# Token and channel weights as float32 in DRAM, VectorE's normalization of the last batch, and a later w_out product

## The chip, the cores and the metric

The kernel runs on one core of one Trainium2 chip. The metric is the device time in microseconds (us) of one execution; each time given for a kernel is the median of several runs. A profile of one further execution gives the trace. In it PE is TensorE, DVE is VectorE, ACT is ScalarE, POOL is GpSimd and SP is SyncE, whose queue issues every DMA of this kernel.

## The reference

Four batches (B = 4) of 576 tokens (S), 8 heads of 64, pass through attention, then through two feed-forward blocks. The weights of the blocks come in float64.

```
scores = q @ k.T / 8; bias = -(cum_i - cum_j)            # cum = cumsum(max(s, 0))
attn = softmax(where(causal, -1e9, scores + min(bias, 0)))
x = attn @ v                                             # (B, 576, 512)
h = gelu_tanh(x @ w_in); u, v = split(h)                 # first block
v_n = (v - mean(v)) / sqrt(var(v) + 1e-6) * g_ln
x = x + (u * (w_sg @ v_n + b_sg)) @ w_out
theta = x @ w_theta                                      # second block
y = w_tok_r @ (x * cos(theta)) + w_tok_i @ (x * sin(theta))
u = x + y
out = u + max(u @ w_ch, 0)
```

## The kernel before

Every product with weights is made of three float32r matmuls, high by high, high by low and low by high, so each weight tensor is kept as a high and a low part in SBUF. A float64 weight is first turned into float32: `to32` takes one ScalarE multiplication and three VectorE operations on its bits (lines 711, 717, 718 and 720). Then `rnd` on ScalarE makes the high part (line 98), and `sub` on VectorE or GpSimd the low part (line 106).

The work has two stretches. In `attention`, pairs of heads `p` = 5 to 16 go by in stages of some 20 us: scores (`sc`), a maximum on VectorE that frees the scores' PSUM (`L417`), the exponential on ScalarE (`L428`), transposes (`T`), and the product with v (`Y`, `Z`). The first block of the batch before (`ffn_in` and `ffn_gate`) is a generator from which `pace` takes matmuls to fill TensorE between them. `PLAN` says in which stage, and at which of four places of it, a piece of a weight is loaded or converted: `R` loads and `W` converts a piece of w_out (first eight) or w_theta, and `W` stores it as float32 to the DRAM tensor `wd`. Their rooms are tiles that the filler does not need yet: `vT` in stages 8 and 12, `vl` and `vh` in stages 9 and 13.

After attention, `ffn_in(3)` and `ffn_gate(3)` of the last batch run alone, the products with w_out (`wout`, matmuls `wo`) of batches 0 and 1 fill in, that of batch 2 follows, and that of batch 3 runs with `theta(0)` (`tp`, `th`). Then `mix` runs (`yo`, `co`). `wout` loads the gated values (`gr`), splits them (`gh`, `gl`; two `gr` and six of each of the others), adds x (`xr`) and stores to `x2d`, from which `theta` loads `x2T`. Meanwhile the generator `second_weights` prepares the second block's weights, one step for every eighth step of `ffn_in(3)` and for every step of `wout`: 8 loads from `wd`, 18 pieces of the token weights (`wk`) and 8 of the channel weights (`wch`) straight from the float64 inputs through `weights64`, which converts each with `to32`. All go through three `wraw` buffers. For the last batch (`alone` in `ffn_in`), `moments` and `norm` follow each of the five row tiles of v; `norm`'s first operation is on GpSimd (line 886).

The order on an engine is set by the program's order and a scheduler that moves instructions between priorities before the kernel is built; on the chip each engine, and SP's queue, runs strictly in that order.

Of the kernel before, what the change touches and what calls it, by code (L numbers as in the profile page):

```python
# [22 lines left out]
P = 128  # L23
# [32 lines left out]
class Kernel:  # L56
# [12 lines left out]

    PLAN = {5: ("C5 L7", "C6", "G0", "C7 G1 B"), 6: ("H0 G2", "H1 G3", "H2 G4", "H3 G5"),  # L70
# [684 lines left out]
    def ffn_weights(self):  # L755
        p = self.f1
        self.wih = self.f3.tile([P, 4, DFF], F32R, name="wih")
        self.wil = self.f3.tile([P, 4, DFF], F32R, name="wil")
        self.wsh = p.tile([P, 4, S], F32R, name="wsh")
        self.wsl = p.tile([P, 4, S], F32R, name="wsl")  # L760
        self.wsrh = p.tile([P, S], F32R, name="wsrh")
        self.wsrl = p.tile([P, S], F32R, name="wsrl")
        self.bsg = p.tile([P, S], F32, name="bsg")
        self.wraw = p.tile([P, 2, FH, 2], U32, name="wraw", tag="vl")
        self.wtab = p.tile([P, 4, FH], F32, name="wtab", tag="vh")
        self.wgt = {}
# [27 lines left out]

    def convert_piece(self, kind, k):
# [6 lines left out]
        elif kind in "RW":  # L802
# [12 lines left out]
            else:  # L815
                raw, ta = self.room[k % 4]
                self.to32(raw.bitcast(U32).rearrange("p (n t) -> p n t", t=2), ta)
                nc.sync.dma_start(self.wd[k // 2, :, h * 256:h * 256 + 256], ta)
        elif kind in "GH":
# [35 lines left out]
    def ffn_in(self, b):  # L855
# [4 lines left out]
        uT = self.f1.tile([P, 4, S], F32, name="uT", tag="uT")  # L860
# [23 lines left out]
        def norm(t):  # L884
            r = TT[t][1]
            nc.gpsimd.tensor_scalar(vT[0:r, t], vT[0:r, t], rs[0:r, t:t + 1], nm[0:r, t:t + 1],  # L886
                                    op0=ALU.mult, op1=ALU.add)
            self.rnd("act", vh[0:r, t], vT[0:r, t])
            if t < 4:
                self.sub("dve", vl[:, t], vT[:, t], vh[:, t])  # L890
            else:
                self.sub("dve", vh[64:128, 4], vT[0:64, 4], vh[0:64, 4])


        for t, (a, r) in enumerate(TT):
# [21 lines left out]
            if t == 4:  # L917

                nc.scalar.copy(uT[0:64, 3, 0:512], o[64:128])
                nc.vector.tensor_tensor(vT[0:64, 4], o[0:64], uT[0:64, 3, 0:512], op=ALU.add)  # L920
# [69 lines left out]
    def wout(self, b, pool):  # L990
        nc = self.nc
        gs = []
        for ft in range(4):
# [6 lines left out]
            gs.append((gh, gl))  # L1000
        for dt in range(4):
# [130 lines left out]
    def run(self):  # L1132
        nc = self.nc
        with ExitStack() as root, ExitStack() as right2, ExitStack() as left2:
# [5 lines left out]
            self.wd = dr.tile([8, P, DM], F32, name="wd")  # L1140
            self.rd = dr.tile([B * H // 2, 2, 5 * P], F32, name="rd")
# [69 lines left out]
    def weights64(self, src, his, los, n):  # L1211

        c = n // 2
        pool = self.stg
        for i in (0, 1):
            raw = pool.tile([P, c, 2], U32, name="wraw", tag="wraw", bufs=3)
            ta = pool.tile([P, c], F32, name="wta", tag="wta", bufs=3)
            for r, w in src:
                self.nc.sync.dma_start(raw[r:r + w.shape[0]].rearrange("p n t -> p (n t)"),
                                       w[:, 2 * i * c:2 * (i + 1) * c])  # L1220
            self.split64(raw, ta, his[:, i * c:(i + 1) * c], los[:, i * c:(i + 1) * c], "pool")
            yield

    def second_weights(self):
# [6 lines left out]
        for k in range(8):  # L1231
            h, l = ((self.woh, self.wol), (self.wth, self.wtl))[k // 4]
            raw = self.stg.tile([P, DM // 2, 2], U32, name="wraw", tag="wraw", bufs=3)
            w = raw.rearrange("p n t -> p (n t)").bitcast(F32)
            self.nc.sync.dma_start(w, self.wd[k])
            self.rnd("act", h[:, k % 4], w)
            self.sub("pool", l[:, k % 4], w, h[:, k % 4])
            yield
        for i in range(9):
            if i < 8:  # L1240
                src = [(0, (self.w_tr, self.w_ti)[i % 2][i // 2 * P:(i // 2 + 1) * P])]
            else:

                src = [(0, self.w_tr[512:576]), (64, self.w_ti[512:576])]
            yield from self.weights64(src, self.wkh[:, i], self.wkl[:, i], S)
        while self.wc is None:
            yield
        self.wch = self.wc.tile([P, 4, DM], F32R, name="wch")
        self.wcl = self.wc.tile([P, 4, DM], F32R, name="wcl")
        for t in range(4):  # L1250
            yield from self.weights64([(0, self.w_ch[t * P:(t + 1) * P])], self.wch[:, t], self.wcl[:, t], DM)
# [46 lines left out]
```

## Time and profile before

| | |
|---|---|
| median of 3 runs | 654.76 us (651.64 to 655.22) |
| the profiled execution | 654.41 us, of which the span of the trace is 652.7 us |
| busy in the span | PE 623.4 us, DVE 423.0 us, ACT 354.5 us, POOL 184.4 us |
| granted TensorE clock | 0.994 of full speed |
| DMA | 83.57 MB |

A share of busy time is an average over stretches with different limits. The rows further down cut the span into stretches; a stretch in which PE is busy for less than its length has a wait in it that something else ended. Matmuls are pipelined, so a matmul's own duration is longer than the distance to the next one.

### The profile page before, as it was taken

The numbers are of one execution on the slowest core, as the hardware profiler recorded it, in microseconds if no ns is written. First come the engines' busy times: TensorE is split into PE (matmuls) and PEld (weight loads), VectorE is DVE, ScalarE is ACT, GpSimd is POOL, SyncE is SP. The second block draws the span as 40 slices with busy tenths as digits, with TensorE's granted clock in tenths as the row PEclk, the third lists the DMA queues.
The fourth block names the chain that finished last, engine by engine and source line by source line (L and its number), as shares of the span: only waits on it lengthen the run. The fifth ranks groups of instructions, "written<-read, shape, count | busy, mean of one in ns | idle before, by whom it ended". The sixth has DMA issues, their size and how long they took to land.

```text
span 652.7 us, 12650 instructions
## 1 busy us (share of the span) xinstructions
PE 623.4 (96%) x4703; PEld 545.9 (84%) x4703; DVE 423.0 (65%) x1048; ACT 354.5 (54%) x829; POOL 184.4 (28%) x213
## 2 busy tenths in 40 slices
PE   9898999899989999999997798999999999999997
PEld 6675777787778878778797797999999899989997
DVE  7896678555674575652299977887663676477422
ACT  5885788656677655771374345655440562256000
POOL 6464424343043440333596534020000100100000
PEclk9999999999999999999998899999999999999999
DMA  6777753565335552112448788621004001300101
GB/s 187 232 246 218 220 162 93 184 224 183 105 107 160 194 176 85 55 38 92 150 126 266 232 302 306 198 95 38 1 1 146 1 1 42 105 1 2 73 1 73
DMA packets 49805, 83.57 MB, mean 128 GB/s; under 512 B 7920, under 2 KB 19792, under 8 KB 49744
## 3 DMA queue, kind: packets, MB, share of 16 engines
q1 hardware_dynamic: 49744, 82.76, 39.4%
q8 instruction: 37, 0.61, 0.4%
q14 instruction: 24, 0.20, 0.1%
HBM read 61.61 MB, written 21.13 MB: 127 GB/s over the span
## 4 chain that ended last, share of the span: by engine, by line
PE 66%; DMA 9%; ACT 7%; DVE 6%; POOL 4%; issue 2%; SPq 0%; DVEq 0%; ACTq 0%; POOLq 0%
PE yo L109 17%; PE fo L109 15%; PE th L109 8%; PE co L109 8%; PE wo L109 5%; PE T L458 4%; PE Y L109 4%; PE sc L109 3%; ACT E L428 2%; POOL vT L886 2%; DMA rd<-rT 2%; DMA xT<-rd 1%; DMA x2T<-x2d 1%; PE tp L1035 1%; DMA x2d<-xr 1%
## 5 line engine op out<-in xcount | busy, mean ns | idle before, releaser
L428 ACT ACTIVATE E<-E,negm 128x192 f32<-128x192 f32 (+4 forms) x160 | 88.4, 555 | 2.7 <-DVE negm L417 2.6
L109 PE MATMUL yo<-wkh,zh 128*128 128x288 f32 x288 | 85.2, 296 | 0.2 <-DVE x2T L1108 0.2
L109 PE MATMUL yo<-wkl,zh 128*128 128x288 f32 x288 | 85.2, 296 | 0.0
L109 PE MATMUL yo<-wkh,zl 128*128 128x288 f32 x288 | 85.2, 296 | 0.0
L417 DVE CUSTOM_DVE_ANT_0 E<-sc,C 128x192 f32<-128x192 f32 (+4 forms) x160 | 68.7, 484 | 2.4 <-PE sc L109 1.6
L458 PE MATMUL T<-ident,E 128*128 128x128 f32 x400 | 55.9, 275 | 7.4 <-DVE xT L525 4.0
L109 PE MATMUL fo<-x,wih 128*128 128x288 f32 x256 | 56.6, 305 | 1.1 <-ACT uT L954 1.1
L458 PEld LDWEIGHTS T<-ident,E 128*128 128x128 f32 x400 | 45.5, 140 | 11.5 <-DVE xT L525 4.4
L102 POOL TENSOR_SCALAR xt<-x2s 128x128 fp32r<-128x128 f32 x16 | 10.8, 690 | 156.5 <-DVE x2s L106 156.5
L109 PEld LDWEIGHTS yo<-wkh,zh 128*128 128x128 f32 x288 | 54.1, 188 | 0.7 <-DVE x2T L1108 0.4
L109 PEld LDWEIGHTS yo<-wkl,zh 128*128 128x128 f32 x288 | 54.1, 188 | 0.3
L109 PEld LDWEIGHTS yo<-wkh,zl 128*128 128x128 f32 x288 | 54.0, 188 | 0.1
L109 PE MATMUL co<-u,wch 128*128 128x288 f32 x256 | 53.0, 295 | 0.0
L109 PE MATMUL wo<-gh,woh 128*128 128x288 f32 x128 | 39.2, 309 | 7.8 <-ACT gh L98 4.1
L109 PEld LDWEIGHTS fo<-x,wih 128*128 128x128 f32 x256 | 41.7, 188 | 3.6 <-ACT uT L954 1.8
L98 ACT CAST u<-x2T 128x576 fp32r<-128x576 f32 x16 | 10.7, 671 | 59.3 <-DVE x2T L1108 59.3
L109 PE MATMUL th<-wth,x2s 128*128 128x512 f32 x128 | 42.9, 400 | 0.0
L468 DVE COPY Ef<-T 128x512 f32<-128x512 f32 x32 | 22.0, 686 | 32.3 <-PE T L458 32.0
L109 PE MATMUL fo<-wih,x 128*128 128x512 f32 x128 | 42.4, 403 | 0.0
L109 PEld LDWEIGHTS co<-u,wch 128*128 128x128 f32 x256 | 41.6, 188 | 0.0
L109 PE MATMUL fo<-wsh,vh 128*128 128x288 f32 x128 | 38.8, 307 | 1.9 <-ACT wsh L98 1.9
L109 PE MATMUL sc<-kh,qh 64*128 64x288 f32 (+1 forms) x192 | 38.9, 365 | 1.3 <-DVE negm L417 1.2
(214 smaller groups left out, 1758.5 us busy)
## 6 DMA issues: line engine op xcount, KB each, us to landing
C<-cd SPq DMA_DIRECT2D x15, 576.0 KB, 4.9
xT<-rd SPq DMA_DIRECT2D x32, 144.0 KB, 3.2
xd<-xT SPq DMA_DIRECT2D x16, 288.0 KB, 4.9
gd<-uT SPq DMA_DIRECT2D x16, 288.0 KB, 2.1
gr<-gd SPq DMA_DIRECT2D x16, 288.0 KB, 4.3
xr<-xd SPq DMA_DIRECT2D x16, 288.0 KB, 3.7
x2d<-xr SPq DMA_DIRECT2D x16, 288.0 KB, 2.5
x2T<-x2d SPq DMA_DIRECT2D x4, 1152.0 KB
```

The lines of the kernel that those rows point to most:

```text
L98: nc.scalar.copy(out, src)
L102: nc.gpsimd.tensor_scalar(out, src, 1.0, 1.0, op0=ALU.mult, op1=ALU.mult)
L109: return self.nc.tensor.matmul(out, lhsT, rhs, start=start, stop=stop)
L417: self.nc.vector.tensor_tensor_reduce(at if j else at[:, ::-1], self.sc[t, j].rearrange("p (b k) -> p b k", k=64), C[:, j, 0:n].rearrange( ...
L428: self.nc.scalar.activation(at, at, AF.Exp, bias=self.negm[pr % 2][:, j, c:c + 1], scale=-1.0, accum_out=sm[:, j * 5 + c:j * 5 + c + 1])
L458: nc.tensor.transpose(T[:, col:col + P], E[:, c:c + P], self.ident)
L468: nc.vector.tensor_copy(Ef[:, 512:1024], T)
L886: nc.gpsimd.tensor_scalar(vT[0:r, t], vT[0:r, t], rs[0:r, t:t + 1], nm[0:r, t:t + 1], op0=ALU.mult, op1=ALU.add)
L1035: nc.tensor.transpose(tp[0:r, dt * P:(dt + 1) * P], x2T[:, dt, a:a + r], self.ident)
```

## The change

- `PLAN` gets pieces `M` (load) and `N` (convert, store) for the 18 pieces of the token weights: three at stage 9, three at 13, four at 15 and eight at 16. The float32 result goes to a new DRAM tensor `wkd`. The first six use the tile `uT` as room; the others use operand, score and raw-load buffers of attention.
- In `ffn_in`, the tile `uT` is therefore taken only ahead of the second half of the matmuls, and the short fifth row tile uses `vT` in place of `uT`.
- `second_weights` begins with converting the 8 channel pieces and storing them to `wcd`; then it loads 8 pieces from `wd`, 9 from `wkd` (576 wide, where there were two of 288) and 4 from `wcd`, and splits each. Its steps are taken at every sixteenth step of `ffn_in(3)` from the 64th on.
- The first operation of `norm` is on VectorE for the last batch.
- `wout` of batch 0 yields a cost of 6000 between its loads and its matmuls.

```
     PLAN = {5: ("C5 L7", "C6", "G0", "C7 G1 B"), 6: ("H0 G2", "H1 G3", "H2 G4", "H3 G5"),
             7: ("H4 G6", "H5 G7", "H6 G8", "H7 G9 H8 H9"),
-            8: ("R0 R1", "R2 R3", "W0 W1", "W2 W3"), 9: ("R4 R5", "R6 R7", "W4 W5", "W6 W7"),
-            12: ("R8 R9", "R10 R11", "W8 W9", "W10 W11"), 13: ("R12 R13", "R14 R15", "W12 W13", "W14 W15")}
+            8: ("R0 R1", "R2 R3", "W0 W1", "W2 W3"), 9: ("R4 R5 M0", "R6 R7 M1 M2", "W4 W5 N0", "W6 W7 N1 N2"),
+            12: ("R8 R9", "R10 R11", "W8 W9", "W10 W11"),
+            13: ("R12 R13 M3", "R14 R15 M4 M5", "W12 W13 N3", "W14 W15 N4 N5"),
+            15: ("M6 M7", "M8 M9", "N6 N7", "N8 N9"),
+            16: ("M10 M11 M12 M13", "N10 N11 M14 M15", "N12 N13 M16 M17", "N14 N15 N16 N17")}
...
+        elif kind == "M":
+            i, h = divmod(k, 2)
+            if k < 6:
+                if k % 3 == 0:
+                    room = self.f1.tile([P, 4 * S], F32, name="wroom", tag="uT")
...
+            for r, w in self.token_rows(i):
+                nc.sync.dma_start(raw[r:r + w.shape[0]], w[:, h * S:h * S + S])
+        elif kind == "N":
+            raw, ta = self.token.pop(k)
+            self.to32(raw.bitcast(U32).rearrange("p (n t) -> p n t", t=2), ta)
+            nc.sync.dma_start(self.wkd[k // 2, :, k % 2 * 288:k % 2 * 288 + 288], ta)
...
-        uT = self.f1.tile([P, 4, S], F32, name="uT", tag="uT")
...
-            nc.gpsimd.tensor_scalar(vT[0:r, t], vT[0:r, t], rs[0:r, t:t + 1], nm[0:r, t:t + 1],
-                                    op0=ALU.mult, op1=ALU.add)
+            (nc.vector if alone else nc.gpsimd).tensor_scalar(
+                vT[0:r, t], vT[0:r, t], rs[0:r, t:t + 1], nm[0:r, t:t + 1], op0=ALU.mult, op1=ALU.add)
...
+        uT = self.f1.tile([P, 4, S], F32, name="uT", tag="uT")
...
+        if b == 0:
+
+            yield 6000.0
...
-                    if n % 8 == 0:
+                    if n % (8 if n < 64 else 16) == 0:
                         self.later(prep)
...
+        for k in range(8):
+            t, h = divmod(k, 2)
+            raw = self.stg.tile([P, S], F32, name="wraw", tag="wraw", bufs=3)[:, 0:DM]
+            ta = self.stg.tile([P, 256], F32, name="wta", tag="wta", bufs=3)
+            nc.sync.dma_start(raw.bitcast(U32), self.w_ch[t * P:(t + 1) * P, h * DM:(h + 1) * DM])
+            self.to32(raw.bitcast(U32).rearrange("p (n t) -> p n t", t=2), ta)
+            nc.sync.dma_start(self.wcd[t, :, h * 256:h * 256 + 256], ta)
             yield
...
+        for k in range(21):
...
+            raw = self.stg.tile([P, S], F32, name="wraw", tag="wraw", bufs=3)[:, 0:n]
+            nc.sync.dma_start(raw, w)
+            self.rnd("act", h, raw)
+            self.sub("pool", l, raw, h)
             yield
```

How the scheduler places this shows in each engine's order. The first place is SP's queue around the start of `ffn_gate(3)`, where `wraw` are weight loads, `gr` and `xr` the loads of `wout`, and `gd` the stores of the gate. Before:

```order
L1219 DMA wraw<-in_moe2_w_tok_r 128x576 x2
L1219 DMA wraw<-in_moe2_w_tok_i 128x576 x2
L1219 DMA wraw<-in_moe2_w_tok_r 128x576
L995 DMA gr<-gd 128x576 x2
L1219 DMA wraw<-in_moe2_w_tok_r 128x576
L1004 DMA xr<-xd 128x576 x3
L1219 DMA wraw<-in_moe2_w_tok_i 128x576
L995 DMA gr<-gd 128x576
```

And with the change:

```order
L1284 DMA wraw<-wd 128x512 x3
L1030 DMA gr<-gd 128x576 x2
L1284 DMA wraw<-wd 128x512
L1042 DMA xr<-xd 128x576 x2
L1284 DMA wraw<-wd 128x512
L1042 DMA xr<-xd 128x576
L1284 DMA wraw<-wkd 128x576
L1030 DMA gr<-gd 128x576 x2
L1022 DMA gd<-uT 128x576
L1284 DMA wraw<-wkd 128x576 x2
```

The loads of `gr` still stand behind weight loads in the queue, but behind loads of float32 pieces, whose buffer is given back by a cast and a subtraction, where it was given back by a whole conversion.

The second place is VectorE at the end of stage 9, where `wtabs` and `wroom` are conversions, `ISA E` the maxima over the scores, and `vT<-fo` the fifth row tile of the filler. Before:

```order
L718 SCALAR_TENSOR_TENSOR wtabs<-wroom,wtabs 128x256 x2
L720 SCALAR_TENSOR_TENSOR wtabs<-wroom,wtabs 128x256
L472 COPY E_72<-T 128x512
L417 ISA E,negm_77<-sc,C 128x9x64
...
L720 SCALAR_TENSOR_TENSOR wtabs<-wroom,wtabs 128x256
L417 ISA E,negm_77<-sc,C 128x576
...
L920 TENSOR_TENSOR vT<-fo,uT 64x512
L468 COPY Ef<-T 128x512
L417 ISA E,negm_77<-sc,C 128x7x64
```

And with the change:

```order
L721 TENSOR_SCALAR wroom<-wroom 128x288
L476 COPY E_74<-T 128x512
L421 ISA E,negm_79<-sc,C 128x9x64
...
L722 SCALAR_TENSOR_TENSOR wtabs<-wroom,wtabs 128x256
L421 ISA E,negm_79<-sc,C 128x192
...
L954 TENSOR_TENSOR vT<-fo,vT 64x512
L722 SCALAR_TENSOR_TENSOR wroom<-wroom 128x288
L472 COPY Ef<-T 128x512
L721 TENSOR_SCALAR wroom<-wroom 128x288
```

Conversions (`wroom`, a token piece, and `wtabs`, a piece of w_out) now stand between the maxima of one group of scores and those of the next.

The third place is TensorE just after the first scores of stage 10, where `fo<-x` are the filler's matmuls of the second half of `ffn_in`. Before:

```order
L109 MATMUL fo<-x,wih 128x288
L109 MATMUL fo<-x,wil 128x288
L458 MATMUL T<-ident,E 128x128 x8
L109 MATMUL fo<-x,wih 128x288 x3
L109 MATMUL fo<-x,wil 128x288 x2
L109 MATMUL fo<-x,wih 128x288 x4
```

And with the change:

```order
L113 MATMUL sc<-mpick,mlow 128x64
L462 MATMUL T<-ident,E 128x128 x19
L113 MATMUL fo<-x,wih 128x288
L113 MATMUL fo<-x,wil 128x288
```

Nineteen transposes stand in a row, without the filler's matmuls that stood between them. Further on, in the last batch, the first matmul of `wout` stands behind 71 of the 112 matmuls of `ffn_gate(3)`, where it stood behind 48.

## Rows read from the trace of the kernel before

**Rows 1.** Stretches of the span: busy us of each engine (instructions), clock, DMA, GB/s.

```profile
core 0: us, PE busy (x) PEld busy (x) DVE busy (x) ACT busy (x) POOL busy (x), PEclk, DMA share, GB/s
128.00:314.70 186.70, 183.43 (x1475) 148.94 (x1473) 107.24 (x332) 113.15 (x293) 60.08 (x68) 1.00 0.38 126
314.70:340.30 25.60, 25.60 (x157) 23.11 (x153) 16.05 (x38) 15.82 (x32) 22.80 (x22) 1.00 0.51 152
340.30:369.20 28.90, 20.79 (x139) 19.63 (x137) 27.75 (x46) 13.46 (x31) 17.93 (x19) 0.94 0.74 236
369.20:400.00 30.80, 28.22 (x195) 27.05 (x195) 23.71 (x53) 13.73 (x30) 11.44 (x15) 0.95 0.92 316
400.00:450.60 50.60, 50.60 (x308) 45.46 (x309) 40.56 (x81) 30.64 (x54) 7.26 (x9) 1.00 0.46 143
```

**Rows 2.** What PE waited for from 340.3 to 400.1: us, times, longest.

```profile
PE wo L109 <- ACT gh L98: 4.1, 2, 3.3
PE wo L109 <- DVE xr L1012: 3.7, 2, 3.3
PE tp L1035 <- ACT x L1038: 1.3, 1, 1.3
PE fo L109 <- DVE vh L106: 0.9, 1, 0.9
```

**Rows 3.** A window of 5 us at the end of that stretch, columns as in rows 1.

```profile
390.00:395.00 5.00, 4.58 (x34) 4.33 (x33) 3.49 (x9) 0.89 (x3) 1.94 (x3) 1.00 1.01 380
```

**Rows 4.** The chain that ended last: start us, length, what.

```profile
387.46 9.26 DMA x2T<-x2d
...
407.48 3.18 PE wo L109 x24
```

**Rows 5.** Conversions (tile `wta`) in the stretch: busy us of DVE, ACT, POOL, then as rows 1.

```profile
340.30:369.20 28.90, 19.78 (x30) 8.59 (x21) 11.04 (x11) 0.94 0.74 236
369.20:400.00 30.80, 12.28 (x28) 7.89 (x19) 8.64 (x10) 0.95 0.92 316
```

**Rows 6.** GpSimd's normalizations (its five on `vT`): ns min/median/max, first and last start.

```profile
L886 POOL TENSOR_SCALAR vT<-vT,rs,nm x5: 782/1044/1774, 329.7 to 339.1; 128x512 f32<-128x512 f32 x4, 64x512 f32<-64x512 f32 x1
```

**Rows 7.** A group of VectorE's operations from 300 to 450: busy us, mean ns, idle before.

```profile
L1064 DVE TENSOR_SCALAR kk<-kk 128x512 f32<-128x512 f32 x7 | 3.1, 441 | 2.2 <-ACT kk L1063 2.2
```

**Rows 8.** A GpSimd and a VectorE instruction side by side: start us, length.

```profile
330.49 1.41 POOL L106 TENSOR_TENSOR wtl<-wraw,wth 128x512 fp32r<-128x512 f32 x1
...
330.77 1.44 DVE L718 SCALAR_TENSOR_TENSOR wta<-wraw,wta 128x288 uint32<-128x288 uint32 x1
```

**Rows 9.** SP's queue at the first `gr` loads: start us, length.

```profile
345.81 0.90 SPq L995 DMA_DIRECT2D gr<-gd  x2
```

**Rows 10.** Conversions during attention (tile `wtabs`; L718 reads like L720): ns min/median/max.

```profile
L711 ACT ACTIVATE wtabs<-wroom x8: 417/432/452, 163.0 to 253.1; 128x256 f32<-128x256 f32 x8
L717 DVE TENSOR_SCALAR wtabs<-wtabs x8: 282/288/289, 168.1 to 254.7; 128x256 uint32<-128x256 uint32 x8
...
L720 DVE SCALAR_TENSOR_TENSOR wtabs<-wroom,wtabs x8: 417/420/422, 169.2 to 257.6; 128x256 uint32<-128x256 uint32 x8
```

**Rows 11.** Windows of 8 us in attention, columns as in rows 1.

```profile
168.00:176.00 8.00, 8.00 (x59) 6.83 (x58) 8.00 (x29) 5.96 (x19) 0.00 (x0) 1.00 0.20 67
184.00:192.00 8.00, 6.39 (x47) 5.92 (x48) 4.42 (x14) 3.81 (x11) 6.66 (x7) 1.00 0.38 111
272.00:280.00 8.00, 7.44 (x65) 6.45 (x64) 7.22 (x19) 7.06 (x21) 4.46 (x5) 1.00 0.01 3
304.00:312.00 8.00, 7.17 (x56) 6.70 (x58) 3.02 (x6) 1.75 (x4) 4.07 (x5) 1.00 0.19 74
```

**Rows 12.** TensorE at 189 us and at 311 us: start us, length, and idle before.

```profile
188.99 0.66 PE L458 MATMUL T<-ident,E 128*128 128x128 f32 x4 [0.97 <-DVE Ef L468]
190.22 0.40 PE L109 MATMUL fo<-x,wih 128*128 128x288 f32 x1 [0.57 <-ACT uT L954]
...
311.47 1.08 PE L109 MATMUL Y<-E,v 128*64 128x512 f32 x4 [0.83 <-ACT E L476]
```

More of the change, by code (lines that the diff above doesn't have):

```diff
@@ L818, in convert_piece @@
                 nc.sync.dma_start(self.wd[k // 2, :, h * 256:h * 256 + 256], ta)
+        elif kind == "M":
[3 more added lines that the diff above has]
+                    room = self.f1.tile([P, 4 * S], F32, name="wroom", tag="uT")
+                    self.half = [(room[:, o:o + S], room[:, t:t + 288]) for o, t in (
+                        (0, 2 * S), (S, 2 * S + 288), (3 * S, 2 * S))]
+                self.token[k] = self.half[k % 3]
+            else:
+                n = ("qh", "ql", "kh", "kl")[(k - 6) % 4]
+                room = self.a2.tile([P, S], F32, name="wroom", tag=n)
+                if k in (6, 10):
+                    tab = self.a1.tile([P, 2 * S], F32, name="wtabs", tag="C", bufs=2)
+                    self.half = [tab[:, t:t + 288] for t in range(0, 2 * S, 288)]
+                elif k in (14, 16):
+                    tab = self.a1.tile([P, S], F32, name="wtabs", tag="QK"[k == 16] + "2")
+                    self.half = [tab[:, t:t + 288] for t in (0, 288)] * 2
+                self.token[k] = room, self.half[(k - 6) % 4]
+            raw = self.token[k][0].bitcast(U32)
+            for r, w in self.token_rows(i):
[4 more added lines that the diff above has]
+            nc.sync.dma_start(self.wkd[k // 2, :, k % 2 * 288:k % 2 * 288 + 288], ta)
         elif kind in "GH":
@@ L917, in ffn_in @@
             if t == 4:
-                nc.scalar.copy(uT[0:64, 3, 0:512], o[64:128])
-                nc.vector.tensor_tensor(vT[0:64, 4], o[0:64], uT[0:64, 3, 0:512], op=ALU.add)
+                nc.scalar.copy(vT[0:64, 4], o[64:128])
+                nc.vector.tensor_tensor(vT[0:64, 4], o[0:64], vT[0:64, 4], op=ALU.add)
                 if alone:
@@ L1209, in run, with second_weights @@
             psl.close()
[L1211 to L1221, printed above, removed]
+    def second_weights(self):
+        nc = self.nc
+        for k in range(8):
[5 more added lines that the diff above has]
+            nc.sync.dma_start(self.wcd[t, :, h * 256:h * 256 + 256], ta)
             yield
-    def second_weights(self):
         p = self.w2
@@ L1230, in second_weights @@
             setattr(self, "wk" + q, p.tile([P, 9, S], F32R, name="wk" + q))
[L1231 to L1237, printed above, removed]
-            yield
[L1239 to L1251, printed above, removed]
+        for k in range(21):
+            if k < 8:
+                n, w = DM, self.wd[k]
+                h, l = (x[:, k % 4] for x in ((self.woh, self.wol), (self.wth, self.wtl))[k // 4])
+            elif k < 17:
+                n, w = S, self.wkd[k - 8]
+                h, l = self.wkh[:, k - 8], self.wkl[:, k - 8]
+            else:
+                while self.wc is None:
+                    yield
+                if k == 17:
+                    wch, wcl = (self.wc.tile([P, 4, DM], F32R, name=n) for n in ("wch", "wcl"))
+                    self.wch, self.wcl = wch, wcl
+                n, w = DM, self.wcd[k - 17]
+                h, l = wch[:, k - 17], wcl[:, k - 17]
+            raw = self.stg.tile([P, S], F32, name="wraw", tag="wraw", bufs=3)[:, 0:n]
+            nc.sync.dma_start(raw, w)
+            self.rnd("act", h, raw)
+            self.sub("pool", l, raw, h)
+            yield
 _INS = ["q", "k", "v", "s", "moe_w_in", "moe_g_ln", "moe_w_sg", "moe_b_sg", "moe_w_out",
```

8 lines of the change are left out of this document (7 added, 1 removed).

## The prediction

> **What bounds the kernel now.** I read the span cut into stretches first, to see where TensorE is not busy; then what it waited for there; then what the engine that ended the waits was doing.
>
> In the stretches [rows 1] TensorE is busy for 183.4 of 186.7 us in the later part of attention, for all of `ffn_in(3)` (314.7 to 340.3), and without a gap from 400.0 to 450.6, where `mix` begins. Between 340.3 and 400.0, the gate of the last batch and more than two `wout` products, it is busy for 49.0 of 59.7 us: the one long hole. VectorE is busy there for 51.5 of 59.7 us, and for 27.75 of 28.9 in the first half. The waits [rows 2] name ScalarE's `gh` (4.1 us), VectorE's `xr` (3.7), ScalarE again ahead of `tp` (1.3; it had itself waited for the transfer of `x2T`) and VectorE's `vh` (0.9). The granted clock is 0.94 and 0.95 in the two halves and 1.00 in the stretches around them, a few us at 1.2 GHz among 2.4.
>
> How much is there to win? The hole holds 139 and 195 matmuls [rows 1], nearly all of the kind of which 24 take 3.18 us in the chain [rows 4], 0.1325 us each. So 334 take 44.3 us, and the hole has 59.7: 15.4 us of waits, of slow clock and of restarts behind waits. That is the most that it can give.
>
> What fills VectorE there is the conversion of token and channel weights: 19.8 + 12.3 = 32.1 us [rows 5]. During attention the same three operations on a piece of 256 columns cost 0.29 + 0.42 + 0.42 = 1.13 us [rows 10], so 1.27 us by columns for a token piece of 288; some in the hole take longer because they are blocked: one of these operations took 1.44 us where a GpSimd subtraction of 1.41 us had begun 0.28 us earlier [rows 8]. And the first `gr` loads, on which `gh` waits, are issued only at 345.8 [rows 9], behind token loads that wait for a buffer that a conversion gives back.
>
> **The change, part by part.**
>
> *Conversions out of the hole.* VectorE's 51.5 us in the hole become 51.5 - 32.1 = 19.4 us of work beside 44.3 us of matmuls: it is no longer the last to arrive. The channel conversions move forward into `ffn_in(3)`: 8 x 1.13 = 9.0 us, and VectorE is idle there for 25.6 - 16.05 = 9.5 us, to which come the first token pieces, which leave it. What is left to wait for in the hole: (a) `gr`, which still stands behind loads of `wd`, whose buffers GpSimd's subtractions give back. The first matmul of `wout` is asked for 23 gate matmuls later (71 for 48; 23 x 0.1325 = 3.0 us), and the wait was 3.3 us at the longest [rows 2]; I leave 1.0 us, bounds 0 and 4.1. (b) `gh` and `gl` at the change from one batch's product to the next, with only two `gr` buffers: 1.5 us, bounds 0 and 3.7 (the `xr` row). (c) `x2T`, which took 9.26 us to land [rows 4] at a DMA share near 1 [rows 3]: 1.5 us, bounds 0 and 4.0 (three times the wait of 1.3). (d) the `vh` wait at the gate's start, below: 0.5 us, bounds 0 and 0.9. Together 4.5 us, so the hole gives 15.4 - 4.5 = 10.9 us. If nothing waits any more it gives 15.4; with all upper bounds (12.7) only 2.7.
>
> *Normalization on VectorE.* Five GpSimd operations of 0.78 to 1.77 us [rows 6] end; on VectorE the nearest row is a `tensor_scalar` of the same shape, 0.44 us [rows 7]. It stands ahead of the last `vh`, on which the gate waited 0.9 us. Bounds: nothing left, or each blocked like the operation in [rows 8], by 1.0 us, 5.0 in all. I take half of the old wait, (d). The Trainium skill speaks against this edit: "SBUF — State Buffer", in the section "SBUF: two separate sides", says that a VectorE operation that takes both ports and a GpSimd operation shut each other out for a whole instruction. The pair in [rows 8] agrees with it.
>
> *Token conversions into attention.* 18 pieces add 18 x 1.27 = 22.9 us to VectorE and, at 0.43 x 288/256 = 0.49 us, 8.8 us to ScalarE [rows 10]. Eight stand in stage 16, where VectorE is busy for 3.0 of 8 us [rows 11]; over the stage's 25 us that covers their 10.2 us. If that cover were gone they would cost the 10.2. Four stand in stage 15 (5.1 us), where VectorE is busy for up to 7.2 of 8 us; but no scores come after these, and the gate's filler keeps TensorE. Six stand at the ends of stages 9 and 13 (3.8 us each), and there VectorE is full: 8.00 of 8 us [rows 11]. Behind them in its queue stand the maxima that free the scores' PSUM and start the exponentials, late by up to 3.8 us; but ScalarE's gelu comes in between, and the second group of exponentials waits for that anyway. More serious is the room: `uT` can't be written before the third piece of the stage has been stored, so both `fo` buffers stay full and nineteen transposes run without filler. Some 24 filler matmuls (3.2 us) come later at each of the two places. Before, TensorE stood there too, 0.97 us for a transposed copy and 0.57 us for `uT` [rows 12], of 1.6 us idle in that window [rows 11]. The deferred filler isn't lost: it fills later stages, and at the end it covers the copy that cost 0.83 us ahead of the last `Y` [rows 12]. I take 1.0 us for each place and 0.8 us back at the end, +1.2 us; bounds -2 (the idle in these rows gone) and 2 x (3.8 + 3.2) = +14.
>
> *SP's queue.* 18 loads (20, as the last piece's two have two halves) and 18 stores, at 0.45 us per issue [rows 9], are 17 us of the queue over four stages of some 20 us. Stores wait for their conversions, and behind them stand `xT` loads and `gd`, some 10 us ahead of their use by the order; I put nothing on it. If that lead were used up, the wait would be one conversion, 1.3 us, for each of the eight of stage 16, 10.2 in all, within the +14.
>
> *`second_weights`* has fewer, wider pieces; its casts and subtractions stay much the same in sum, and it is done long before 450.6, where `mix` needs the last of it: nothing, and if it were late, up to one load, 4 us.
>
> **Sum.** The profiled execution took 654.4 us (652.7 of span and 1.7 around it): 654.4 - 10.9 + 1.2 = 644.7. It lies 0.3 us under the median of the runs, so the sum stands for either. I predict 644.5 us. From 400 on TensorE is full and its matmuls stay the same; that part only moves forward.
>
> **Rivals.**
> 1. *Transfers bound the hole.* Its second half moves 316 GB/s at a share of 0.92, and its end 380 at 1.01 [rows 1, 3]. All of it, 28.9 x 236 + 30.8 x 316, 16.6 MB, in 48.8 us would be 339 GB/s. That is below 380, so it speaks for late transfers, not for a limit. With (a) to (c) at 9.3 us and (d) at 0.5 the gain is 5.6 and the time 654.4 - 5.6 + 1.2 = 650.
> 2. *GpSimd's subtractions block the normalization*, 5.0 us at the gate's start in place of 0.5: 644.7 + 4.5 = 649. For it: [rows 8]. Against it: the first four row tiles are done several us ahead of the gate. The Trainium skill's rule, named above, would have it wherever the two engines meet.
> 3. *Attention pays* (slower): the filler held back by the `uT` room, with the maxima behind the conversions. At 7 us a place, with stage 15's 5.1 us open too, attention loses 19.1: 654.4 - 10.9 + 19.1 = 662.6. It makes up for the hole from 5.5 us a place, and is over 0.5% slower from 7.1. For it: VectorE's full window. Against it: ScalarE sets the pace behind the gelu, and TensorE's work is only put off.
> 4. *Hardly anything waits any more*: (a) to (d) at 1 us, attention even: 640.
>
> **How the numbers follow.** Half a per cent, 3.3 us, is about what runs of this kernel can tell from no change. My forecast, 641 to 649, has 0.60. Rival 1 has 0.15 (0.10 below 651.5, 0.05 above), rival 2 0.05, rival 4 0.08, rival 3 0.12, of which 0.05 ends beyond 658 and 0.07 within half a per cent. Faster: 0.60 + 0.10 + 0.05 + 0.08 = 0.83; same 0.05 + 0.07 = 0.12; slower 0.05. The range reaches from rival 4 to the edge of rival 1, 639.5 to 651.5; it leaves out 0.17 above and a little below.
>
> **What would show it.** The way from the gate's start to the gapless part should take about 49 us in place of 59.7, with VectorE clearly below full, the two waits of 3.3 us gone and the clock at 1.00; the last `Z` of attention should end within 2 us of its place at 314.7. I am wrong if TensorE's idle time around stages 9 to 10 and 13 to 14 grows by several us, if `wo` waits for `gr` or `x2T` at a DMA share of 1, or if `fo` waits for `vh` at the gate's start by more than it did.

## The result, and the profile after

The changed kernel takes 658.79 us (median of 9 runs, 654.95 to 661.54), the kernel before 654.76 us (9 runs, 651.53 to 656.16): a ratio of 1.0064, 95% interval 1.0041 to 1.0087. It is slower, where 644.5 us was forecast. The profiled execution took 658.41 us with a span of 656.7 us, 4.0 us more than the span of before.

The stretches of the span after the change, columns as in [rows 1]. The first ends with the last `Z` of attention, the second with the first gate matmul on `vl`, the fifth with the first `yo` of `mix`:

```profile
128.00:318.00 190.00, 184.11 (x1462) 148.99 (x1462) 123.61 (x375) 118.01 (x310) 59.90 (x68) 0.99 0.50 161
318.20:344.10 25.90, 25.90 (x158) 23.42 (x156) 16.67 (x49) 10.99 (x24) 6.50 (x8) 1.00 0.52 167
344.10:360.00 15.90, 10.64 (x55) 9.82 (x54) 8.01 (x16) 7.43 (x14) 11.38 (x11) 0.68 0.74 241
360.00:400.00 40.00, 37.32 (x271) 35.65 (x269) 20.89 (x30) 16.31 (x27) 26.37 (x22) 1.00 0.92 308
400.00:452.20 52.20, 51.44 (x313) 46.21 (x314) 37.29 (x71) 28.84 (x49) 4.20 (x7) 1.00 0.42 137
452.20:656.70 204.50, 199.41 (x1413) 192.15 (x1411) 113.57 (x208) 73.60 (x127) 5.06 (x8) 1.00 0.10 37
```

Attention ends 3.5 us later than before. VectorE did become free in the hole: busy 8.0 + 20.9 of 55.9 us, where it was 51.5 of 59.7 [rows 1]. TensorE waits there all the same, and the clock of the gate's stretch is 0.68. What it waited for from 300 to 470 us:

```profile
PE fo L113 <- DVE vh L110: 3.7, 1, 3.7
PE yo L113 <- DVE zl L110: 1.3, 2, 1.2
PE fo L113 <- ACT vh L102: 1.2, 1, 1.2
PE wo L113 <- ACT gh L102: 1.1, 2, 0.9
PE wo L113 <- DVE xr L1050: 1.0, 2, 0.8
PE wo L113 <- DVE gl L110: 1.0, 1, 1.0
```

The two waits of 3.3 us in [rows 2] are gone, and `vh`, which was 0.9 us there, is 4.9. The chain that ended last shows what came between the fifth row tile's gelu (`vT L956`) and its last `vh`:

```profile
340.45 0.45 ACT wta L715
340.89 0.52 ACT vT L956
...
342.86 1.54 DVE wta L722
...
345.18 4.13 DMA wraw<-wd
...
349.33 0.62 ACT woh L102
349.95 0.53 ACT vh L102
...
350.50 1.35 DVE vh L110
...
351.90 1.33 PE fo L113 x4
```

Windows of 5 us there, columns as in [rows 1]. Behind the window in which TensorE is busy for 1.64 of 5 us, it runs at 0.50, its lower level of 1.2 GHz, for a whole window. At 0.74 a full window holds 31 matmuls, at 1.00 it holds 40. A wait costs here twice, once as a wait and once as a clock:

```profile
345.00:350.00 5.00, 1.64 (x7) 0.91 (x5) 1.94 (x6) 2.21 (x5) 1.82 (x2) 0.74 0.73 214
350.00:355.00 5.00, 3.10 (x13) 3.10 (x14) 1.86 (x2) 2.96 (x7) 4.54 (x4) 0.50 0.66 206
355.00:360.00 5.00, 5.00 (x31) 5.00 (x30) 3.31 (x4) 2.25 (x4) 5.00 (x5) 0.74 0.99 347
360.00:365.00 5.00, 5.00 (x40) 5.00 (x39) 3.27 (x4) 2.86 (x5) 5.00 (x5) 1.00 0.97 350
```

And a place that the forecast did not have, the chain where `mix` begins. The last `wout` product stands right ahead of it, with only four `theta` matmuls behind; `zh` starts 0.02 us after the product's end, because its buffers lie in the room that `wout` gives back, and `zl` comes behind it. The last line is of ScalarE's timeline: it sat idle for 6.09 us until that product was done.

```profile
448.21 2.67 PE wo L113 x20
450.87 0.02 issue
450.89 3.23 ACT zh L102 x6
454.13 0.67 DVE zl L110
...
457.26 2.66 PE yo L113 x18
```

```profile
450.89 4.26 ACT L102 CAST zh<-zf 128x512 fp32r<-128x512 f32 x8 [6.09 <-PE wo L113]
```

Before, 20 matmuls of `theta` stood there (16 `th` and 4 transposes `tp`). TensorE's order, before and then with the change (`wo` is the end of the product, `yo` is `mix`):

```
L109 MATMUL wo<-gl,woh 128x288
L109 MATMUL th<-wth,x2s 128x512 x2
L109 MATMUL th<-wtl,x2s 128x512
L109 MATMUL th<-wth,x2s 128x512 x2
...
L109 MATMUL th<-wth,x2s 128x512
L109 MATMUL yo<-wkh,zh 128x288
```

```
L113 MATMUL wo<-gl,woh 128x288
L113 MATMUL th<-wth,x2s 128x512 x2
L113 MATMUL th<-wtl,x2s 128x512
L113 MATMUL th<-wth,x2s 128x512
L113 MATMUL yo<-wkh,zh 128x288
```

### The profile page after: what moved, and what is told of

It reads as the page before. It is cut to its first block, busy times and chain, and to the rows that moved or that the text cites. A ratio compares the mean times of both kernels' runs of the same rounds, so it can differ in the third digit from the quotient of the medians.

```text
span 656.7 us, 12688 instructions
## 1 busy us (share of the span) xinstructions
PE 627.4 (96%) x4703; PEld 548.7 (84%) x4703; DVE 418.5 (64%) x1053; ACT 351.9 (54%) x816; POOL 173.1 (26%) x195
## 4 chain that ended last, share of the span: by engine, by line
PE 74%; DVE 10%; DMA 6%; ACT 5%; issue 3%; POOL 1%; SPq 1%; ACTq 0%; DVEq 0%; POOLq 0%
PE fo L113 19%; PE yo L113 17%; PE th L113 8%; PE co L113 8%; PE wo L113 7%; PE Y L113 5%; PE sc L113 5%; PE T L462 4%; DVE E L421 3%; DMA wraw<-in_moe_w_ch 2%; PE tp L1073 1%; ACT E L432 1%; DMA x2d<-xr 1%; DVE stats L911 1%; DMA wkd<-wroom 1%
## 5 line engine op out<-in xcount | busy, mean ns | idle before, releaser
L462 PE MATMUL T<-ident,E 128*128 128x128 f32 x400 | 58.4, 280 | 6.5 <-DVE xT L529 3.7
L113 PE MATMUL fo<-x,wih 128*128 128x288 f32 x256 | 58.3, 308 | 2.4 <-ACT uT L989 2.4
L113 PEld LDWEIGHTS fo<-x,wih 128*128 128x128 f32 x256 | 43.1, 192 | 5.5 <-ACT uT L989 3.1
L113 PE MATMUL fo<-wsh,vh 128*128 128x288 f32 x128 | 40.6, 320 | 3.4 <-ACT wsh L102 2.2
L1020 POOL TENSOR_TENSOR uT<-gt,uT 128x288 f32<-128x288 f32 x32 | 29.4, 925 | 46.6 <-DVE gt L1018 33.1
```

The lines of the kernel that those rows point to most:

```text
L113: return self.nc.tensor.matmul(out, lhsT, rhs, start=start, stop=stop)
L462: nc.tensor.transpose(T[:, col:col + P], E[:, c:c + P], self.ident)
L1020: nc.gpsimd.tensor_tensor(uT[:, ft, a:a + m], gt, uT[:, ft, a:a + m], op=ALU.mult)
```

## The experiments

Three lengths, each from one profiled execution, describe every kernel: A, from the `Z` matmuls near 180 us to the last `Z` of attention; G, from the gate's first matmul on `vl` to the first `yo`; M, from there to the end of the span. A spell of low clock, such as the one in [rows 1] (28.9 us at 0.94), adds to one of them: the changed kernel's two profiles differ by 1.7 us in A and by 1.7 in G. The mean clock of G is 1.00 in E8, E14 and E16 alone, and 0.94 to 0.98 in all others. A profiled execution can also lie far from its kernel's median (E1's is 650.75 us for 656.02, E9's 661.24 for 655.86); the stretch ahead of A alone takes 176.9 to 182.4 us. So a difference of less than 2 us in A or G tells nothing by itself; M repeats better (204.5 and 204.6). The ratio is to the kernel before on the same chip, with its 95% interval.

| kernel | median us | ratio | A | G | M |
|---|---|---|---|---|---|
| before | 654.76 | | 134.4 | 109.8 | 202.3 |
| changed | 658.79 | 1.0064 (1.0041 to 1.0087) | 139.7 | 108.1 | 204.5 |
| E19 changed again | 660.51 | 1.0097 (1.0077 to 1.0117) | 138.0 | 109.8 | 204.6 |
| E1 GpSimd normalizes | 656.02 | 1.0030 (1.0005 to 1.0055) | 137.6 | 106.1 | 202.2 |
| E2 channel late | 658.80 | 1.0075 (1.0050 to 1.0100) | 138.0 | 111.7 | 202.5 |
| E3 w_out not later | 657.88 | 1.0067 (1.0040 to 1.0095) | 139.7 | 108.3 | 204.5 |
| E4 tokens only | 655.08 | 1.0005 (0.9977 to 1.0033) | 137.9 | 108.4 | 202.5 |
| E5 no early pieces | 657.65 | 1.0056 (1.0034 to 1.0077) | 139.3 | 106.1 | 204.8 |
| E7 one channel load | 664.68 | 1.0155 (1.0130 to 1.0180) | 139.7 | 111.8 | 202.3 |
| E8 VectorE subtracts | 655.38 | 1.0001 (0.9979 to 1.0023) | 137.8 | 106.0 | 204.4 |
| E9 E8, channel late | 655.86 | 1.0017 (0.9992 to 1.0041) | 139.8 | 105.4 | 205.9 |
| E10 E1, channel late | 655.42 | 1.0015 (0.9998 to 1.0032) | 138.3 | 107.3 | 202.5 |
| E11 E10, eight steps | 656.58 | 1.0033 (1.0008 to 1.0057) | 138.0 | 109.2 | 202.4 |
| E12 E9, eight steps | 654.43 | 0.9991 (0.9968 to 1.0014) | 138.0 | 104.3 | 205.1 |
| E13 no late pieces | 655.63 | 1.0014 (0.9991 to 1.0037) | 139.3 | 106.6 | 202.0 |
| E14 before, eight steps | 656.43 | 1.0022 (1.0002 to 1.0043) | 134.4 | 110.9 | 202.3 |
| E15 E12, no early pieces | 652.95 | 0.9974 (0.9954 to 0.9994) | 139.6 | 103.6 | 202.5 |
| E16 E12, no late pieces | 651.98 | 0.9962 (0.9938 to 0.9987) | 137.8 | 105.5 | 202.4 |
| E17 E12, one token load | 650.58 | 0.9939 (0.9914 to 0.9965) | 139.7 | 99.1 | 202.9 |
| E18 E12, GpSimd's queue | 658.11 | 1.0056 (1.0036 to 1.0076) | 137.8 | 108.9 | 202.7 |

**What holds the gate.** E1, the normalization back on GpSimd:

```
-            (nc.vector if alone else nc.gpsimd).tensor_scalar(
+            nc.gpsimd.tensor_scalar(
```

> The changed kernel with one edit undone: GpSimd normalizes the last batch again. In the changed kernel the gate's first products wait 5.3 us for `vh` (1.2 + 0.3 + 3.7), and the clock is low for 15 us behind it. Theory A (channel conversions, which each wait for a transfer, stand between the normalization's steps in the in-order queues of ScalarE and VectorE): the engine of the five normalizations is not the cause; the waits stay at 4.5 us or more and the time within 0.4% of the changed kernel, 657 to 661 us. Theory B (VectorE's normalization, blocked by GpSimd's subtractions, holds up `vh`): the waits fall to about 1 us, as before the change, and the time to 651 to 654 us.

E2, the channel weights last:

```
-        for k in range(8):
...
-            nc.sync.dma_start(self.wcd[t, :, h * 256:h * 256 + 256], ta)
-            yield
...
+        for k in range(8):
...
+            self.split64(raw.bitcast(U32).rearrange("p (n t) -> p n t", t=2), ta, wch[:, t, c], wcl[:, t, c], "pool")
+            yield
```

> The changed kernel with the channel weights converted last, straight from float64 into their tables, as before the change; token conversions stay in attention and VectorE still normalizes. Theory A: the gate's waits for `vh` fall from 5.3 to under 1.5 us, the clock behind them stays at 1.00, and the first gate matmul comes at 343 to 345 us in place of 346.4; the eight conversions come back into the hole behind the gate, 9 us of VectorE where it has room: 650 to 654 us. Theory B: the waits stay above 4 us, 657 to 661 us. In both the last `Z` of attention stays at 317 to 319 us.

E7, eight channel conversions of one load:

```
-            nc.sync.dma_start(raw.bitcast(U32), self.w_ch[t * P:(t + 1) * P, h * DM:(h + 1) * DM])
+            if k == 0:
+                raw = self.stg.tile([P, DM], F32, name="wone", tag="wone", bufs=1)
+                nc.sync.dma_start(raw.bitcast(U32), self.w_ch[0:P, 0:DM])
```

> The changed kernel, with one load of channel weights in place of eight: the eight conversions all work on the first piece, so that their operations and stores stay in place and only the transfers that they wait for are gone (the channel weights, and so the last part of the output, are then not the reference's). Theory A in its form 'the waits for transfers in in-order queues do it': the gate's waits for `vh` fall to under 2 us and the time to 650 to 655 us. Its rival 'the work itself, 9 us of VectorE and 3.4 us of ScalarE ahead of the normalization, does it': the waits stay at 4 us or more and the time at 657 to 660 us.

E1 came out between its theories: the `vh` waits fell from 4.9 to 2.2 us and the time by some 3 us, not to 651 to 654. Of the time, 2.3 us can be M, which became 202.2, so E1 alone shows little of what the normalization is worth. E2 was level with the changed kernel (its G is 3.6 us longer and its M 2.0 shorter): though the channel loads had gone from the chain, TensorE still waited 4.4 us for `vh`. E7, without the waits for seven of them, lost 6 us more: VectorE was busy for all of 330 to 350 us (14.2 of these 20 us in the changed kernel), its conversions stood between the steps of the normalization, several took 1.5 us beside GpSimd's subtractions, and the first `gr` load was issued at 358.68 us instead of 351.69. So theory A falls as the one cause. E2's trace shows one that is left, on VectorE (first fence) and GpSimd (second): start us, length.

```profile
342.40 0.15 DVE L914 TENSOR_SCALAR mv<-mv 128x1 f32<-128x1 f32 x1
...
343.60 1.35 DVE L916 SCALAR_TENSOR_TENSOR nm<-mv,rs 128x1 f32<-128x1 f32 x1 [0.44 <-POOL rs L915]
344.98 1.58 DVE L920 TENSOR_SCALAR vT<-vT,rs,nm 64x512 f32<-64x512 f32 x1
```

```profile
343.54 2.75 POOL L110 TENSOR_TENSOR wkl<-wraw,wkh 128x576 fp32r<-128x576 f32 x2
```

Beside GpSimd's two subtractions, an operation on one element a partition takes 1.35 us and the normalization 1.58; in E8, where GpSimd subtracts nothing, they take 0.15 and 0.53. ScalarE's last `vh` waited 2.6 us for that. The Trainium skill, "SBUF — State Buffer", section "SBUF: two separate sides", says that the engine that comes first holds the shared ports for its whole instruction; these rows agree.

E8 takes GpSimd's subtractions away, E9 has the channel weights last as well (E2's edit), and E10 is E1 with E2's edit:

```
-            self.sub("pool", l, raw, h)
+            self.sub("dve", l, raw, h)
```

> The changed kernel with one operation on another engine: the low halves of the second part's weights (`wol`, `wtl`, `wkl`, `wcl`) are subtracted on VectorE in place of GpSimd, so that GpSimd runs nothing long beside the normalization. Theory B (VectorE's steps of the normalization are stretched because GpSimd's subtractions run beside them; with channel weights late they took 1.3 to 1.7 us in place of 0.15 to 0.55): the gate's waits for `vh` fall from 5.3 us to under 2 us and the time to 653 to 656 us. Theory A' (the order in the queues: casts and conversions that wait for their loads stand ahead of the normalization's steps on ScalarE and VectorE, whoever subtracts): the waits stay at 4 us or more, 657 to 660 us.

> The same as the kernel with VectorE's subtractions, and the channel weights converted last as before the change. Theories A' and B, each with a share: the last `vh` is done by 344 us, about when before the change, the waits for it are under 1.5 us and the time 651 to 654 us. If what is behind the gate takes over (the `gr` loads are issued behind the weights' loads, and `gh` waits 4 us, as it did with channel weights late alone), the gain of the gate is given back and the time is 655 to 658 us.

> The changed kernel with two edits undone: GpSimd normalizes the last batch, and the channel weights are converted last. GpSimd then works off subtractions and normalizations in the order of its own queue, and nothing of VectorE's in the normalization but four short operations a row tile can be stretched. Theory B with A': waits for `vh` of 1 us as before the change, and 650 to 654 us. If only the order on ScalarE counts: as with channel weights late alone, waits of 4 us and 657 to 660 us.

E8's time was in theory B's range and level with before, and its normalizations took 0.53 to 0.54 us, though 3.0 us of waits for `vh` were left, above the 2 expected. The clean pair is E2 and E10, which differ in the normalization's engine alone: M is the same, and E10 is 0.6% faster, with intervals that do not overlap. E8 gains as much on the changed kernel with M unchanged. So whether GpSimd normalizes or VectorE subtracts, 3 to 4 us come back. E9 came out as its second expectation had it, `vh` at 1.0 us and `gh` at 4.1; E10 ended 1.4 us above its better one. The place of the channel weights adds nothing that these runs can tell. Theory A' keeps a share: in E8, as in the chain of the changed kernel above, the cast of a `wd` piece (`woh`) that waits for its load stands on ScalarE right ahead of the last `vh`.

**What holds the hole.** E4, tokens alone: E1's, E2's and E3's edits, and

```
-                    if n % (8 if n < 64 else 16) == 0:
+                    if n % 8 == 0:
```

> The kernel before with the token conversions alone moved into attention: GpSimd normalizes, the channel weights are converted last from float64, `w_out`'s product stands where it stood, and the pieces of the second part's weights are issued as often as before the change. If the moved conversions are worth what the forecast gave them and attention costs 3.5 us: 654.8 - 10.9 + 3.5 = 647 us. If attention's cost and the later waits for `gh` eat it up: 653 to 657 us. Against the kernel with the same two edits undone and `w_out`'s product later, it shows what that later place is worth: more than 1.5 us either way would be seen.

E11 (on E10) and E12 (on E9) issue eight steps of `second_weights` ahead of the gate; E14 does so to the kernel before:

```
-                    if n % (8 if n < 64 else 16) == 0:
+                    if n % 8 == 0 and n < 64:
```

> The kernel with GpSimd's normalization and channel weights last, and only eight steps of `second_weights` (the `wd` pieces, which the first `wout` product needs) issued before the gate in place of fourteen; the rest follow between `wout`'s products. Theory D (what holds the gate and the hole is what stands ahead of the last `vh` and of the first `gr` load in the in-order queues): the first `gr` load goes out at 341 to 343 us instead of 348.8, waits for `vh` and `vl` fall from 3.3 to under 1 us, and the time is 649 to 653 us. Theory E (the transfers themselves bound the hole, near a DMA share of 1): the same bytes go through the same engines, the waits move to `gh` and `xr`, and the time stays at 654.5 to 657 us.

> The same eight steps, with VectorE normalizing and subtracting in place of GpSimd, channel weights last. Theory D: as with GpSimd's normalization, 649 to 653 us, and if stretched operations beside GpSimd were still part of it, 1 us less. Theory E: 654.5 to 657 us.

> The kernel before, with one number changed: eight steps of `second_weights` ahead of the gate in place of nineteen, so that no token conversion stands there; all conversions stay where they were otherwise, from float64. Theory D: the first `gr` load goes out at 340 to 342 in place of 345.8 us, the waits for `gh` (4.1 us) and `vh` (0.9) go, VectorE has to do the eleven steps later in the hole, and the time is 649 to 653 us. Theory F (VectorE is the bound of the hole, as the forecast had it): the waits move to `gl` and `xr`, 654 to 657 us.

E4 is the forecast's main step alone, and G went from 109.8 to 108.4 us only. Its hole, then its waits there:

```profile
343.40:400.00 56.60, 46.27 (x319) 44.87 (x319) 35.45 (x64) 23.11 (x46) 29.25 (x30) 0.94 0.76 251
```

```profile
PE wo L113 <- DVE xr L1047: 6.6, 2, 5.2
PE fo L113 <- DVE vh L110: 2.0, 1, 2.0
PE fo L113 <- DVE vl L110: 1.3, 1, 1.3
```

VectorE is idle for 21 us of 56.6, and TensorE still stands for 10. The longest wait, 5.2 us, is for the addition that `xr` names. It stood in VectorE's queue behind a conversion of channel weights, for which ScalarE waited 5.4 us until its load had landed:

```profile
379.05 5.71 DMA wraw<-in_moe_w_ch
...
384.84 0.44 ACT wta L715
...
386.80 0.38 DVE xr L1047
...
387.22 11.13 PE wo L113 x72
```

E11 stayed where theory E put it (`vh` and `vl` 3.5 us, `xr` 6.8), and the first `gr` load went out at 345.8 us, not at 341 to 343. E14 ended in theory F's range; VectorE is as full there as before, so it can't tell F from E, and it is E4 that speaks against F. E12's 654.43 us are just below its theory E: with no stretched operation and fewer steps ahead of the gate, G is 104.3, and 3 us of it go again in M.

E17 leaves eight of nine token loads out of E12, E18 moves the loads of `second_weights` to GpSimd's queue:

```
+            if k < 8:
+                raw = self.stg.tile([P, S], F32, name="wraw", tag="wraw", bufs=3)[:, 0:n]
+            elif k == 8:
+                raw = self.stg.tile([P, S], F32, name="wone", tag="wone", bufs=1)
+            if k <= 8:
+                nc.sync.dma_start(raw, w)
```

```
-            nc.sync.dma_start(raw, w)
+            nc.gpsimd.dma_start(raw, w)
```

> The kernel with VectorE's subtractions and eight steps ahead of the gate, with eight of the nine loads of token tables left out: all nine casts work on the first one (so the token weights, and the output, are not the reference's). It takes 2.3 of some 14.5 MB out of the hole, and eight places in SP's queue. Theory E (the transfers, or the loads ahead of `gr` in SP's queue, bound the hole): the first `gr` load goes out at 342 us or earlier, the waits for `gh` (4.1 us) and `vh` (1.4) halve, and the first `yo` comes 3 to 5 us earlier after the gate's start than the 104.3 us of that kernel. Theory G (the chain at the change of batch: product, cast, subtraction, then the next load into one of two `gr` buffers): the wait of 3.5 us for `gh` stays, and the first `yo` comes within 1.5 us of that. TensorE's order ahead of `mix` is the good one, so 2 us may come from there in either case.

> The kernel with VectorE's subtractions and eight steps ahead of the gate (654.4 us), with the loads of `second_weights` issued on GpSimd's queue in place of SP's. The bytes stay. TensorE's order ahead of `mix` becomes the good one, which is worth 2.3 us by itself, so 652 us if nothing else changes. If SP's in-order queue is what the loads cost (E1), the first `gr` load goes out at the gate's start instead of 3.8 us behind it, and the kernel comes near the one without eight of the loads: from the gate's start to the first `yo` 99 to 101 us, 649 to 651 us. If it is the bytes (E2): 102.5 to 105 us, 652 to 654.5 us.

(In E18's text, E1 and E2 stand for two forms of theory E, not for the runs of these names.) What TensorE waited for, first in E12, then in E17:

```profile
PE wo L113 <- ACT gh L102: 4.1, 2, 3.5
```

```profile
PE wo L113 <- DVE xr L1050: 3.0, 1, 3.0
```

E17's G is 99.1 us, 5.2 less than E12's, theory E; 1.2 us of it only moved ahead of the gate, as from the last `Z` to the first `yo` it is 126.5 us for 130.4. The wait for `gh` is gone, so it was no chain of buffers (G); the one for `xr` that is left stands again behind a channel conversion whose load is late. By the ratios E17 is 3.4 us faster than E12, and M makes up 2.2 of that, so what the loads are worth lies between 1 and 4 us. E17 takes out their bytes, their places in SP's queue and the waits of eight casts together, and can't tell these apart. The first `gr` load goes out at the gate's start, though late by the clock (344.92). In E18 it goes out at the gate's start too, and its bytes are E12's:

```profile
341.02 0.80 SPq L1030 DMA_DIRECT2D gr<-gd  x2
```

G is nevertheless 108.9, above both ranges. A `wkd` load issued at 341.89 us, beside the `gr` and `xr` loads, landed 5.9 us later; its cast stands ahead of the last `vh` on ScalarE, which waited 3.7 us for it, and TensorE 3.7 us for `vh`. So a free SP queue is not enough, which speaks for the bytes; but each load now also occupies GpSimd for 0.54 us, so E18 doesn't settle it. (The same section of the Trainium skill warns that a DMA from GpSimd's queue can starve while VectorE holds the ports; no run here separates that.)

**What attention pays.** E5 has no pieces at stages 9 and 13, E13 none at 15 and 16; `second_weights` converts theirs from float64 (E5's lines; E13 has `11 <= k < 17`):

```
-            13: ("R12 R13 M3", "R14 R15 M4 M5", "W12 W13 N3", "W14 W15 N4 N5"),
+            13: ("R12 R13", "R14 R15", "W12 W13", "W14 W15"),
...
+            if 8 <= k < 11:
...
+                    self.split64(raw.bitcast(U32).rearrange("p (n t) -> p n t", t=2), ta, h[:, c], l[:, c], "pool")
```

> The changed kernel without the six token pieces at the ends of stages 9 and 13 (the ones that borrow the room of `uT`); these six are converted straight from float64 in the hole instead. Theory C (the borrowed room holds back the filler, and attention pays): the last `Z` comes back from 318.0 to 314 to 315.5 us, TensorE's idle time in 176 to 192 us falls from 4.0 to about 1.7 us, and since the gate's stall stays the time is 654.5 to 657 us. The rival (the pieces of stages 15 and 16 delay attention, or the stretch before it only scattered): the last `Z` stays at 317 us or later and the time at 658 to 661 us.

> The changed kernel without the twelve token pieces of stages 15 and 16, which are converted straight from float64 in the hole; the six at the ends of stages 9 and 13 stay. From the `Z` at 180 us to the last `Z` attention takes 134.4 us before the change, 139.7 after it, and 139.4 without the six early pieces. If the late pieces are what attention pays for: 134 to 136 us. If each place costs only where the filler is gone, and early pieces alone cost as much by holding the filler back: 137 to 140 us. Time: the hole gets 12 conversions back, the gate stays late: 656 to 660 us.

Neither brings A back; E14, whose attention is that of the kernel before, has its 134.4 us. No run takes out both sets and keeps the later `uT`, so what that edit costs by itself is not shown. What TensorE waits for in the changed kernel from 176 to 192 us, and in E15 (which has no early pieces either) from 288 to 319 us:

```profile
PE fo L113 <- ACT uT L989: 2.0, 1, 2.0
PE T L462 <- DVE xT L529: 1.5, 1, 1.5
PE T L462 <- DVE Ef L472: 0.5, 1, 0.5
```

```profile
PE Y L113 <- ACT wtabs L715: 2.2, 1, 2.2
PE fo L113 <- DVE gt L1018: 1.2, 1, 1.2
```

With the early pieces TensorE loses 4.0 us at stage 9, where it lost 1.6 [rows 11]; the filler that they put off then covers the late pieces (105 matmuls from 304 to 318 us, against 78 in E15). Without them, the late pieces stand open. So, as far as single profiles show it, each set costs about what both do: A is 137.8 us in E16, which has the early pieces alone and no spell of low clock, as in E8, which has both. That E13 was faster than the changed kernel by 0.5% lies in G and M.

**The order ahead of `mix`.** E15 and E16 are E12 without the early and the late pieces; the order of TensorE ahead of `mix` ends with `theta` again. E15's edit is E5's on E12, E16's is:

```
-            15: ("M6 M7", "M8 M9", "N6 N7", "N8 N9"),
-            16: ("M10 M11 M12 M13", "N10 N11 M14 M15", "N12 N13 M16 M17", "N14 N15 N16 N17")}
...
+            if 11 <= k < 17:
```

> The kernel with VectorE's subtractions, eight steps ahead of the gate and channel weights last (654.4 us), without the six token pieces of stages 9 and 13, which are converted straight from float64 in the hole. The order of instructions on TensorE ahead of `mix` becomes that of before: 24 `wout` products, then 15 of `theta`, then `mix`. Theory H (the `wout` product that stands last delays `mix` by 2 to 3 us): the stretch from the first `yo` to the end falls from 205.1 to 202 to 202.6 us and the time to 651 to 653 us. If that order only moves a wait from one place to another: 654 to 656 us.

> The same kernel, without the twelve token pieces of stages 15 and 16 instead; the six early ones stay. TensorE's order ahead of `mix` again ends with products of `theta`. Theory H: 202 to 202.6 us from the first `yo` to the end. Twelve conversions go back into the hole, 15 us of VectorE by the rows of attention, and VectorE was busy there for 39 of 60 us: covered, 651 to 653.5 us; if it becomes the last to arrive again, as before the change, 654 to 657 us.

M fell from 205.1 to 202.5 and 202.4 us, as theory H has it, and both are faster than the kernel before (by 0.3 and 0.4%) and than the changed one; E16 is the fastest here that leaves no work out. Over all kernels the split is clean: M is 204.4 to 205.9 us in the seven that have a `wout` product with at most four `theta` matmuls ahead of `mix` (changed, E3, E5, E8, E9, E12, E19), and 202.0 to 202.9 in the thirteen others. Which order the scheduler makes hangs on edits far from there.

E3 takes out the later place of w_out's product, E19 changes nothing:

```
-        if b == 0:
-
-            yield 6000.0
```

> The changed kernel without the edit that lets `w_out`'s first product stand further on. The order on TensorE ahead of `mix` is as bad as in the changed kernel with or without it. If the later place is worth the wait for `gr` that the forecast spoke of (3 us), this kernel is slower by that, 661 to 662 us; if gate and product wait for other things anyway, it is within 1.5 us of the changed kernel, 657 to 660 us.

> The changed kernel again, unaltered. If what the profile of its first run showed is the kernel's own: waits for `vh` of 4 to 6 us at the gate's start with a low clock behind them, a wait for `zl` of 1.2 us ahead of `mix`, 204 to 205.5 us from the first `yo` to the end, and a ratio of 1.004 to 1.009. If it was the scatter of runs: waits under 3 us, and a ratio below 1.003.

E3 is level with the changed kernel: the later place is worth nothing that can be told. E19 shows the same waits (`vh` 5.7 us, `zl` 1.2) and a larger loss.

## Why the prediction was wrong

- **"It is no longer the last to arrive"; the hole gives 10.9 us.** This step failed. VectorE was freed as counted, but what TensorE waited for was late for other reasons: with the token conversions gone and 21 of 56.6 us idle on VectorE (E4), TensorE still stood for 10 us, the longest time behind one conversion whose load was late. The freed VectorE gave 1.4 us (E4), within the scatter, in place of 10.9. The matmuls would fit about as the forecast said: from the last `Z` to the first `yo` E17 takes 126.5 us, 9.5 less than before. Going by single profiles, 1.4 of these are E4's, 4.0 came with what else E12 has (above all no subtractions on GpSimd and fewer steps ahead of the gate), and 4.0 with eight loads less; E17's median puts these nearer to 1. Rival 1 named the transfers and got 0.15, and its price, a gain of 5.6 us with 9.3 us for (a) to (c) that no row gives, was too good as well. I set it aside because 339 GB/s lay below a window's 380, which says nothing of single loads that come late at the head of a queue. Whether bytes or places in queues make them late stays open.
- **(d), normalization on VectorE, 0.5 us.** It was 5.2 us with `vl` in the profile, of which 2.8 come back in E1 and 1.9 in E8. Rival 2 priced it at 5.0 and got 0.05; its argument against, that the first row tiles are done early, missed that the last one goes from ScalarE to VectorE, GpSimd, VectorE, ScalarE and VectorE again, each time behind whatever `second_weights` has queued there. That GpSimd's subtractions stretch it, the mechanism of rival 2, is what E2, E8 and E10 show.
- **Channel conversions, "8 x 1.13 = 9.0 us, and VectorE is idle there".** The sum of busy time was no cover; yet E2 shows that moving them back alone gains nothing that can be told.
- **Attention, +1.2 us.** A grew by 3.6 us (E19), with a spell of low clock 5.3 (the changed kernel). The mechanism, `uT` and the filler that is put off, was as described; the size was not: 4.0 us of waits at stage 9 against the 1.0 us a place that I took.
- **"From 400 on TensorE is full and its matmuls stay the same."** The number did stay, 1413 matmuls from the first `yo` on, but M grew by 2.2 us through the order ahead of `mix`, which I didn't compare; no term or rival had it.
- **Clock at 1.00.** It fell to 0.68 in the gate's stretch, behind the new wait.

In the profile: 5.3 us lost in A, 1.7 gained in G, 2.2 lost in M, and 1.8 ahead by 180 us, where nothing had changed: the 4.0 us. The place of `w_out`'s product, by which (a) counted the first matmul 3.0 us later, is worth nothing that can be told (E3). How much of E18's loss is GpSimd's issuing stays open.

## What to carry to other kernels

An engine that is full beside a stall is not yet what the stall waits for: before pricing the work taken off it, ask what else in that stretch is late, here loads of weights and the in-order queues behind them. Work that is issued early "beside idle time" stands in in-order queues; follow the last row tile through every engine and count what is ahead of it at each. And when a scheduler sets the order, compare the whole order, also where the change edits nothing.

## What the runs showed of the hardware

A VectorE operation on 128x1 took 1.35 us beside GpSimd's subtraction, nine times its 0.15 us alone, so short operations pay the most in proportion. A DMA issued on GpSimd's queue held that engine for 0.54 us, on SP's queue an issue takes 0.32 to 0.51 us (E12).
